# Causal attention into a maxout feed-forward layer: the last query block's two heads transposed by one issue

## The chip, the core and the metric

One core of one Trainium2 chip runs the whole program. The metric is the device time of one execution in microseconds (us); several executions are timed and the median is given. Five engines work side by side: TensorE (PE in the profile; its weight loads are PEld), VectorE (DVE), ScalarE (ACT), GpSimd (POOL) and SyncE (SP), whose queue here issues nearly all the DMA transfers. Each takes its instructions in order, and waits on semaphores for the others.

## The reference, cut to what matters

```python
def attn(q, k, v, s):                      # B, H, S, D = 8, 8, 576, 64
    scores = q @ k^T / sqrt(D)
    cum = cumsum(max(s, 0))
    scores = where(causal, -1e9, scores + min(-(cum[i] - cum[j]), 0))
    p = softmax(scores)                    # with + 1e-9 in the sum
    return p @ v
x = attn(...) as (B*S, H*D) = (4608, 512)
h = max(x @ w1, x @ w2, x @ w3)            # d_ff = 768
out = h @ w_out                            # (4608, 512), float32
```

## The kernel before, in words

**Visits and steps.** Two heads of a batch (a pair) are worked on together; one pair's stay is a visit, and a visit goes through blocks of 128 query rows, one block a step (the last block, number 4, has 64 rows). There are 160 steps: first blocks 0 and 1 of the eight pairs of batches 0 and 1, then their blocks 2, 3 and 4, then all five blocks of the 24 pairs of batches 2 to 7 (the "stacked" visits, with float16 high and low parts of q and k in tiles `h` and `l`). In every step TensorE computes scores two steps ahead, VectorE the row maxima (L738), ScalarE the exponentials, and `probs` (L791) divides by the row sum and splits the result into a float16 high part (`prh`, written by ScalarE) and a low part (`prl`, written by VectorE).

**Transposes.** The product with the values needs the probabilities with the keys on the partitions, so `probs` has SyncE issue DMA transposes into `ph` and `pl`: two issues (high, low) for block 1 (L835), two each for blocks 2 and 3 (L840), and four for block 4 (L846). There the 128 partitions hold 64 rows of each head, and each part of each head is an issue of its own: 64 partitions by 4 blocks (high) or 5 (low, which carries the 64 keys beyond 512 of both parts).

**Values.** `values` (L963) multiplies for a half of a visit: 256 query columns (blocks 0, 1), or 320 (blocks 2, 3, 4) in 28 matmuls. Each takes a 128 x 64 weight tile of one head, so matmuls come in pairs, head 0 and head 1 in different columns of the array. All high parts times the high and low values come first, then the low parts. It runs at the end of the step after the half's last `probs`.

**Feed-forward.** As soon as a batch's half is complete, `add_set` queues 18 up-products (groups of 12 matmuls, L1116, 256 or 320 columns) and 4 down-products (groups of 18, L1158); their results go out by a ScalarE copy (L1166) and one store each (L1167). Batch 0's first half runs in float32 (L1187, L1209). `PLAN["GROUPS"]` says how many groups are run at two places of each step, 309 in all; the rest runs after the last step.

**Order.** Everything else (loads, splits, weight decoding, scales) is put by hand into the list of a step: `at` (L1277) appends to the work at the step's end, shifted by `PLAN["moved"]`, `soon` (L1264) puts it before the scores. Scales need a maximum over the partitions: `power` (L515) is one matmul on a VectorE result (`ambv`, `ambwd`), whose product VectorE reads later. `keep_on` (L908) issues matmuls that compute nothing, as many as `PLAN["KEEP"]` says. For stacked visits `nat_hi`/`nat_lo` (L236, L239) write q and k parts into a staging tile (`fixed`), `nat_own` copies one head's part on the same partitions, and `nat_far` (L268) moves the other by DMA, separately for `h` and `l`.

Of the kernel before, what the change touches and what calls it, by code (L numbers as in the profile page):

```python
# [47 lines left out]
('load_nat', 26): -2, ('nat_far', 38, 1, 0): 1, ('load_nat', 28): -1, ('nat_hi', 24, 0): 1, ('load_nat', 21): -1,
('prep2', 0): -2, ('decode4', 21): 2, ('nat_bias', 36, 0): -1, ('pair_max', 18, 1): 1, ('prep4', 22): -1, ('decode3',
17): -1, ('load_nat', 27): 1, ('nat_bias', 25, 1): 2, ('nat_far', 28, 0, 0): 1, ('prep2', 3): 1, ('prep2', 11): 1,  # L50
('vmax', 39): 1, ('nat_own', 20, 0, 1): 1, ('nat_bias', 22, 1): 2, ('load_v', 31): 1, ('load_nat', 36): -1,
('nat_bias', 35, 1): -2, ('nat_far', 35, 1, 1): 1, ('nat_bias', 38, 1): 1, ('nat_bias', 29, 1): 1, ('nat_hi', 17, 0):
-1, ('prep4', 24): -1, ('prep5', 14): -1, ('nat_hi', 16, 0): -1, ('prep5', 38): 1, ('nat_far', 32, 1, 1): 1,
('nat_own', 31, 0, 1): 1, ('pair_scale1', 2): -1, ('nat_hi', 28, 0): 1, ('nat_far', 32, 1, 0): -1, ('nat_far', 35, 0,
0): -1, ('nat_far', 36, 1, 1): 1, ('bias4', 0): 1, ('nat_far', 21, 1, 1): 1, ('decode4', 22): 1, ('prep4', 35): -2,
('load_w', 10): -1, ('nat_hi', 35, 0): 1, ('load_w', 7): 1, ('nat_hi', 27, 0): -1, ('nat_bias', 24, 0): 1, ('prep3',
6): -1, ('prep5', 24): -1, ('pair_scale3', 4): 1, ('load_nat', 35): -2, ('load_nat', 39): 1, ('nat_own', 35, 1, 0): 2,
('nat_hi', 33, 0): 1, ('nat_bias', 23, 1): 1, ('nat_far', 31, 1, 1): -1, ('prep4', 23): 1, ('nat_far', 29, 1, 0): -1,
('nat_own', 28, 1, 1): 1, ('prep4', 15): -1, ('load_v', 22): -1, ('load_nat', 32): 1, ('load_v', 10): 1, ('nat_far',
35, 1, 0): -1, ('sign', 2): 1, ('sign', 15): 1, ('nat_bias', 26, 1): -1, ('nat_far', 21, 0, 1): 1, ('nat_bias', 28,  # L60
1): -1, ('nat_own', 23, 1, 1): 2, ('prep4', 27): -1, ('load_w', 5): -1, ('nat_far', 28, 1, 0): 1, ('prep4', 9): 1,
('nat_far', 34, 0, 1): -1, ('nat_far', 17, 1, 1): -1, ('prep4', 10): 1, ('nat_bias', 17, 1): -1, ('load_w', 8): -1,
('nat_own', 32, 1, 1): 1, ('nat_own', 31, 1, 1): 1, ('prep2', 15): -1, ('pair_max', 25, 1): 1, ('nat_far', 32, 0, 0):
1, ('prep4', 33): -2, ('prep3', 4): 1, ('decode3', 12): -1, ('prep4', 28): -1, ('prep4', 26): 1, ('nat_hi', 32, 0): 1,
('nat_hi', 18, 1): -1, ('nat_hi', 31, 0): -1, ('nat_own', 27, 0, 1): 1, ('prep4', 38): 2, ('load_nat', 24): -1,
('nat_far', 34, 0, 0): 1, ('vmax', 19): -1, ('prep5', 19): -1, ('pair_max', 17, 0): 2, ('prep4', 29): -1, ('nat_far',
24, 1, 0): -1, ('prep4', 34): -2, ('nat_far', 36, 0, 1): 1, ('vmax', 6): 1, ('nat_bias', 25, 0): -1, ('vmax', 29): 1,
('nat_lo', 38, 1): 1, ('nat_own', 23, 0, 1): 1, ('nat_lo', 29, 0): -1, ('load_nat', 33): -1, ('decode1', 2): -1,
('nat_bias', 31, 1): 1, ('nat_own', 19, 1, 1): 1, ('load_nat', 29): 1, ('prep5', 5): -1, ('prep5', 39): -1,
('nat_far', 18, 0, 1): -1, ('nat_far', 31, 0, 1): -1, ('decode3', 7): -1, ('nat_hi', 39, 1): 1, ('load_v', 26): -1,  # L70
('load_w', 23): -1, ('nat_own', 23, 1, 0): 1, ('nat_bias', 20, 1): 1, ('nat_far', 34, 1, 0): 1, ('gram1', 0, 5): 1,
('nat_hi', 37, 1): 1, ('nat_lo', 34, 0): -1, ('nat_bias', 29, 0): -1, ('nat_far', 37, 1, 1): -1, ('pair_max', 16, 0):
1, ('nat_hi', 21, 0): -1, ('nat_own', 20, 1, 1): 1, ('load_nat', 38): 1, ('nat_lo', 18, 0): -1, ('load_v', 23): -1,
('vmax', 4): -1}),
# [4 lines left out]
"fetched": ({5: 0, 7: -1, 8: 0, 9: 0, 10: -2, 11: 2, 12: 2, 13: 0, 14: 1, 15: 2, 16: 2, 17: 0, 22: 3, 23: 4, 18: 4, 19: 5, 20: 8,  # L79
21: 6}),  # L80
"GROUPS": ([(0, 0), (0, 0), (0, 0), (0, 0), (0, 0), (0, 0), (0, 0), (0, 0), (0, 2), (0, 2), (1, 3), (0, 1), (0, 0), (0, 2), (1,
# [11 lines left out]
"FIRST": (0),  # L93
"KEEP": ({('b', 37): 2, ('d', 69): 10, ('b', 70): 18}),
"EX": ((0, 1, 2)),
"EX0": ((0, 1, 2, 3, 4)),
}
# [1440 lines left out]
```

## Time and profile before

| | us |
|---|---|
| median of 3 runs (846.43 to 849.97) | 848.02 |
| the profiled execution | 846.36 |
| its span, first to last instruction | 844.5 |
| TensorE busy / VectorE / ScalarE / GpSimd | 807.6 / 638.5 / 532.5 / 296.2 |
| granted clock of TensorE, mean | 0.994 |

Busy time is the union of an engine's instructions, so what is left of the span is idle time of that engine. The profiled execution takes 1.9 us more than its span. A matmul's recorded length contains its pipeline and is longer than the distance to the next one's start; distances between starts show the rate.

### The profile page before, as it was taken

To read this page: it belongs to the slowest core of one execution; us is meant where nothing else is said; L and a number is where in the kernel's file an instruction comes from. 1 tells how busy PE (TensorE), PEld (TensorE's weight loads), DVE (VectorE), ACT (ScalarE), POOL (GpSimd) and SP (SyncE) were. 2 spreads that over 40 slices of the span, in tenths; PEclk is the share of its full clock that TensorE was granted. 3 is DMA by queue.
4 is the path that set the end of the run, shared out by engine and by line. 5 is a ranking of instruction groups with operands and counts; after the bars stand their busy time and mean duration, and the time that the engine had idled before them with its cause. 6 is when DMAs were issued, how large, how long until landed. Compare 5 with 4: busy or idle time off the path is not lost.

```text
span 844.5 us, 19376 instructions
## 1 busy us (share of the span) xinstructions
PE 807.6 (96%) x6959; PEld 619.5 (73%) x6959; DVE 638.5 (76%) x1562; ACT 532.5 (63%) x1458; POOL 296.2 (35%) x532
## 2 busy tenths in 40 slices
PE   5889899899999989999999999999999999999998
PEld 3777678777676668777787678777877688778875
DVE  6889988889778888898887879877978787662110
ACT  5878777496577676766775666665766576652111
POOL 1001114757433333254434524362335335221221
PEclk9999899999999999999999999999999999999999
DMA  9933377896877696867886678656787665443000
GB/s 351 378 87 84 84 170 184 184 157 138 160 171 135 127 199 144 172 123 169 186 156 131 124 166 184 137 135 132 143 181 121 128 119 116 92 78 71 19 8 32
DMA packets 236672, 119.82 MB, mean 142 GB/s; under 512 B 208800, under 2 KB 217504, under 8 KB 236576
## 3 DMA queue, kind: packets, MB, share of 16 engines
q1 hardware_dynamic: 236000, 117.01, 63.4%
q10 hardware_dynamic: 576, 1.57, 0.5%
q8 instruction: 55, 0.90, 0.5%
q14 instruction: 41, 0.34, 0.2%
HBM read 45.12 MB, written 9.44 MB: 65 GB/s over the span
## 4 chain that ended last, share of the span: by engine, by line
PE 70%; DVE 11%; DMA 8%; ACT 5%; issue 2%; POOL 2%; SPq 1%; ACTq 0%; DVEq 0%; POOLq 0%
PE pm L1116 40%; PE po L1158 13%; PE av L983 6%; PE s L644 5%; DMA pl<-prl 3%; DVE prl L832 2%; DMA r<-in_w_dram 2%; PE s L656 1%; ACT prh L829 1%; PE pm L1187 1%; DVE w L1089 1%; DMA raw<-in_start_dram 1%; PE po L1209 1%; DMA rv<-in_qkv_dram 1%; ACT e L779 1%
## 5 line engine op out<-in xcount | busy, mean ns | idle before, releaser
L1116 PE MATMUL pm<-x,w 128*128 128x320 f16 (+1 forms) x3240 | 422.4, 287 | 0.9 <-DVE x L994 0.7
L1116 PEld LDWEIGHTS <-w 128*128 128x128 f16 x3240 | 312.2, 98 | 90.2 <-issue 3.5
L829 ACT ACTIVATE prh<-e,ri 128x128 f16<-128x128 f32 (+3 forms) x200 | 96.7, 529 | 95.5 <-DVE ri L807 93.3
L1133 DVE SCALAR_TENSOR_TENSOR m<-pm,m 128x320 f32<-128x320 f32 (+1 forms) x180 | 82.0, 456 | 93.1 <-PE pm L1116 82.6
L1122 POOL CAST hh<-m 128x320 f16<-128x320 f32 (+1 forms) x90 | 46.0, 511 | 298.7 <-DVE m L1133 233.0
L1158 PE MATMUL po<-hh,w 128*128 128x320 f16 (+1 forms) x720 | 140.6, 287 | 0.0
L1158 PEld LDWEIGHTS <-w 128*128 128x128 f16 x1080 | 103.7, 98 | 30.1 <-issue 1.7
L832 DVE SCALAR_TENSOR_TENSOR prl<-e,ri,prh 128x128 f16<-128x128 f32 (+3 forms) x200 | 110.5, 591 | 8.9 <-ACT prh L829 5.7
L748 DVE CUSTOM_DVE_ANT_0 s<-s,later,qf 128x128 f32<-128x128 f32 (+1 forms) x192 | 103.7, 550 | 14.3 <-PE s L644 11.5
L779 ACT ACTIVATE e<-s,nm 128x128 f32<-128x128 f32 (+4 forms) x216 | 105.6, 497 | 5.4 <-DVE nm L748 2.5
L1158 PE MATMUL po<-hl,w 128*128 128x320 f16 (+1 forms) x360 | 103.2, 287 | 0.2 <-POOL hl L1123 0.2
L266 POOL COPY h<-fixed 64x576 f16<-64x576 f16 x96 | 73.2, 778 | 83.2 <-DVE fixed L241 79.2
L1130 ACT ACTIVATE m<-pm 128x320 f32<-128x320 f32 (+1 forms) x90 | 36.4, 405 | 72.5 <-PE pm L1116 69.2
L1123 POOL TENSOR_TENSOR hl<-m,hh 128x320 f16<-128x320 f32 (+1 forms) x90 | 68.7, 764 | 7.4
L829 ACT ACTIVATE prh<-s,ri 128x512 f16<-128x512 f32 x72 | 46.7, 684 | 31.7 <-DVE ri L807 31.6
L1166 ACT ACTIVATE o<-po,os 128x320 f32<-128x320 f32 (+1 forms) x60 | 29.9, 499 | 50.1 <-PE po L1158 44.3
L983 PEld LDWEIGHTS <-vh 128*64 128x64 f16 x800 | 44.9, 110 | 22.3 <-issue 15.4
L832 DVE SCALAR_TENSOR_TENSOR prl<-s,ri,prh 128x512 f16<-128x512 f32 x72 | 51.8, 748 | 8.4 <-ACT prl L829 8.2
L983 PE MATMUL av<-ph,vh 128*64 128x320 f16 (+3 forms) x368 | 48.6, 281 | 1.4 <-DMA ph<-prh 1.4
L779 ACT ACTIVATE s<-s,nm 128x512 f32<-128x512 f32 (+1 forms) x72 | 48.4, 673 | 0.0
L644 PE MATMUL s<-h 128*128 128x128 f16 (+1 forms) x192 | 42.3, 300 | 3.4 <-DVE prl L832 1.8
L241 DVE SCALAR_TENSOR_TENSOR fixed<-fixed,qf,fixed 128x576 f16<-128x576 f32 x48 | 40.6, 881 | 4.7 <-ACT fixed L237 4.7
(210 smaller groups left out, 1202.8 us busy)
## 6 DMA issues: line engine op xcount, KB each, us to landing
fixed<-in_pair_dram SPq DMA_DIRECT2D x24, 576.0 KB, 4.7
r<-in_w_dram SPq DMA_DIRECT2D x22, 512.0 KB, 8.4
rv<-in_qkv_dram SPq DMA_DIRECT2D x32, 320.0 KB, 3.7
h<-fixed SPq DMA_DIRECT2D x48, 144.0 KB, 2.7
l<-fixed SPq DMA_DIRECT2D x48, 144.0 KB, 2.8
out_dram<-o SPq DMA_DIRECT2D x32, 160.0 KB, 2.0
out_dram<-o SPq DMA_DIRECT2D x32, 128.0 KB, 1.9
raw<-in_qkv_dram SPq DMA_DIRECT2D x8, 480.0 KB, 3.9
```

The lines of the kernel that those rows point to most:

```text
L266: nc.gpsimd.tensor_copy(out=R[v]["h"][own, j, x], in_=staged(v)[own, 3 - x])
L644: nc.tensor.matmul(ps[:, j, :nk], lhsT=w[:, c, qs], rhs=w[:, 1 - c, 0:nk], start=(x == "h" and not (lone and j)), stop=(x == "l"), skip_gr ...
L748: nc.vector.tensor_tensor_reduce(out=sc[:, j], in0=sc[:, j], in1=future[0][:, Q4 - nk:Q4], scale=n, scalar=3.0e38, op0=ALU.add, op1=ALU.mi ...
L779: nc.scalar.activation(out=to, in_=sc, func=AF.Exp, bias=nm[:, j:j + 1], scale=-1.0 if below(t) else 1.0, accum_out=sm[:, j:j + 1],)
L829: nc.scalar.activation(out=hi, in_=src, func=AF.Copy, scale=sc)
L832: nc.vector.scalar_tensor_tensor(out=lo, in0=src, scalar=sc, in1=hi, op0=ALU.mult, op1=ALU.subtract)
L983: nc.tensor.matmul(av[j * D:(j + 1) * D, c0:nq] if ph else av[j * D:(j + 1) * D, c0:nq].rearrange("p (i c) -> p i c", c=P), lhsT=lt, rhs=r ...
L1116: nc.tensor.matmul(pm[:, :nq], lhsT=w[:, wt, kt, :], rhs=xt, start=(n == 0), stop=(n == 3 * NKT - 1))
L1122: nc.gpsimd.tensor_copy(out=st["hh"][:, ft, :nq], in_=m1[:, :nq])
L1123: nc.gpsimd.tensor_tensor(out=st["hl"][:, ft, :nq], in0=m1[:, :nq], in1=st["hh"][:, ft, :nq], op=ALU.subtract)
L1133: nc.vector.scalar_tensor_tensor(out=m1[:, :nq], in0=pm[:, :nq], scalar=HSC, in1=m1[:, :nq], op0=ALU.mult, op1=ALU.max)
L1158: nc.tensor.matmul(pm[:, :nq], lhsT=W[18 + ft][:, wt, dt, :], rhs=st[ht][:, ft, :nq], start=(n == 0), stop=(n == 3 * NFT - 1),)
```

## The change

1. **Last block.** `probs` puts both parts of both heads of block 4 into one tile `pr` of 128 x 9 x 128, transposed by one issue into `pT2`; `values` takes the first 256 columns from `ph`, `pl` and then the last 64 from `pT2`, in matmuls of their own: 52 in place of 28.
2. **Far copies.** `h` and `l` of a stacked visit become one tile `lh`; `nat_far` moves both in one issue, at the place of the second.
3. **Stores.** Two down-products share a tile and a store, except in the last set.
4. **Scales.** The `power` matmul of the down weights, and of the values' scale for the visits before the stacked ones, moves from the end of a step to before the scores of the next.
5. **Order.** 60 entries of `moved`, 50 steps of `GROUPS` (309 groups as before), five of `fetched`, and `KEEP` at one step from 10 matmuls to 2.

```diff
-"KEEP": ({('b', 37): 2, ('d', 69): 10, ('b', 70): 18}),
+"KEEP": ({('b', 37): 2, ('d', 69): 2, ('b', 70): 18}),
...
     def nat_far(v, j, x):
+        if not x:
+            return
         own, far = slice(j * D, (j + 1) * D), slice((1 - j) * D, (2 - j) * D)
-        nc.sync.dma_start(out=R[v]["hl"[x]][far, j], in_=staged(v)[own, 1 - x:3 - x])
+        u = staged(v)[own, 0:2]
+        two = bass.AP(tensor=u.tensor, offset=u.offset, ap=[list(u.ap[0]), [S, 2], [1, 2 * S]])
+        nc.sync.dma_start(out=R[v]["lh"][far, :, j].rearrange("p y i c -> p y (i c)"), in_=two)
...
+        elif qb == 4:
+            both = att.tile([P, 9, P], F16, tag="pr4", name=f"pr{t}", bufs=1)
+            halves = [both[:, 0:4], both[:, 4:9]]
...
         elif ph:
-            for c in range(2):
-                for j in range(2):
-                    nc.sync.dma_start_transpose(
-                        out=pT[c][:, 0:8 + 2 * c, 256:320].rearrange("p (n j) c -> p n j c", j=2)[:, :, j, :],
-                        in_=halves[c][j * D:(j + 1) * D, 0:4 + c, :].rearrange("p n c -> p (n c)"),
-                    )
+            nc.sync.dma_start_transpose(out=PT[v, 2], in_=both.rearrange("p n c -> p (n c)"))
...
-                        rt = pT[t][:, 2 * kb + j, c0:nq] if ph else pT[t][:, j + 4 * kb:j + 3 + 2 * kb:2, :]
-                        todo.append((j, r[vt][:, j, kb, :], rt, c0))
+                        rt = pT[t][:, 2 * kb + j, c0:2 * P] if ph else pT[t][:, j + 4 * kb:j + 3 + 2 * kb:2, :]
+                        todo.append((j, r[vt][:, j, kb, :], rt, c0, 2 * P))
         if ph:
+            pT = PT.pop((v, 2))
+            for part in parts:
+                for kb in range(4):
+                    for vt, t in part:
+                        for j in range(2):
+                            todo.append((j, r[vt][:, j, kb, :], pT[:, 4 * t + kb, j * D:(j + 1) * D], 2 * P, nq))
...
-        WS[kind] = power(clamp(am, f"w{kind}"), f"w{kind}")
+        WS[kind] = clamp(am, f"w{kind}")
...
+        if kind == "d" and PLAN["WP"]:
+            soon(end + 1, wscale_power, kind)
...
-        if v < 2 * NP * NB + NP:
+        if v < 2 * NP * NB + NP and PLAN["VP"]:
+            soon(first[v] + 1, vscale_power, scale_of(v))
```

**SyncE's queue at the first stacked visit**, before (`fixed<-in_pair_dram` is a load; the rest as named above):

```order
L840 DMA_TRANSPOSE ph_2712<-prh_2786 128x8x128
L840 DMA_TRANSPOSE pl_2713<-prl_2787 128x8x128
L230 DMA fixed_2854<-in_pair_dram 128x1152
L846 DMA_TRANSPOSE ph_2712<-prh_2884 128x4x64 x2
L846 DMA_TRANSPOSE pl_2713<-prl_2885 128x5x64 x2
L209 DMA rv_2919<-in_qkv_dram 128x640
L270 DMA h_2748<-fixed_2684 64x1152
L270 DMA l_2749<-fixed_2684 64x1152
```

and now:

```order
L856 DMA_TRANSPOSE ph_2802<-prh_2898 128x8x128
L856 DMA_TRANSPOSE pl_2803<-prl_2899 128x8x128
L235 DMA fixed_2951<-in_pair_dram 128x1152
L860 DMA_TRANSPOSE pT_2979<-pr_2982 128x9x128
L214 DMA rv_3012<-in_qkv_dram 128x640
L279 DMA lh_2837<-fixed_2718 64x2x1152 x2
```

Four issues of the last block have become one, and the four far copies (the `h` and `l` rows come twice, once a head) two; the neighbours kept their places.

**TensorE at the scale of the down weights** (`gmwd`; the gram product L1044 that it measures is done), before:

```order
L699 MATMUL s_1092<-kb_180,qr_183 128x384 x2
L703 LDWEIGHTS identb
L703 MATMUL s_1092<-tri,identb 128x128
L519 LDWEIGHTS ambwd
L519 MATMUL gmwd<-identb,ambwd 128x128
L1187 MATMUL pm_0_4_0_1125<-x_0_327,r_361 128x256 x2
L1187 MATMUL pm_0_4_0_1125<-x_0_558,r_361 128x256 x2
```

and now:

```order
L714 MATMUL s_1091<-tri,identb 128x128
L1217 MATMUL pm_0_4_0_1121<-x_0_328,r_362 128x256 x2
L1217 MATMUL pm_0_4_0_1121<-x_0_557,r_362 128x256 x2
L1001 MATMUL av<-ph_939,vh_933 64x256
L1001 MATMUL av<-pl_940,vh_933 64x128
L529 MATMUL gmwd<-identb,ambwd 128x128
L710 MATMUL s_1153<-qk_979 128x512 x6
```

The small matmul that waits for VectorE now stands behind a float32 product of four matmuls and the 12 matmuls of a values half (of which two rows stand for all).

**TensorE's values of a second half**, before, the low parts' last rows:

```order
L983 MATMUL av<-pl_1832,vh_1817 64x320
L983 MATMUL av<-pl_1832,vh_1817 64x192
L983 MATMUL av<-pl_1832,vh_1817 64x64
L983 LDWEIGHTS vl_1818
L983 MATMUL av<-pl_1832,vl_1818 64x64
```

and now:

```order
L1001 MATMUL av<-pl_1920,vh_1868 64x256
L1001 MATMUL av<-pl_1920,vh_1868 64x128
L1001 MATMUL av<-pT_2125,vh_1868 64x64
L1001 LDWEIGHTS vl_1869
L1001 MATMUL av<-pT_2125,vl_1869 64x64
```

The 24 matmuls of 320 or 192 columns have 256 or 128, and 24 of 64 columns, each with a weight load of its own, stand behind them with the four that were there.

## Rows read from the trace of the kernel before

**Rows 1.** Stretches of the span: length, busy us (instructions) per engine, clock, DMA share, GB/s

```profile
core 0: us, PE busy (x) PEld busy (x) DVE busy (x) ACT busy (x) POOL busy (x), PEclk, DMA share, GB/s
0.00:50.00 50.00, 36.04 (x245) 29.53 (x246) 40.02 (x89) 35.41 (x107) 4.21 (x25) 0.97 0.81 309
50.00:130.00 80.00, 72.04 (x460) 57.81 (x458) 68.90 (x151) 59.71 (x154) 10.35 (x12) 0.96 0.50 122
130.00:345.00 215.00, 204.39 (x1839) 154.42 (x1837) 182.13 (x415) 145.34 (x392) 102.54 (x177) 1.00 0.79 158
345.00:772.00 427.00, 426.07 (x3863) 323.12 (x3862) 335.93 (x885) 283.15 (x791) 164.72 (x292) 1.00 0.68 139
772.00:844.50 72.50, 69.07 (x562) 54.64 (x559) 11.49 (x25) 8.84 (x20) 14.36 (x26) 1.00 0.05 17
```

**Rows 2.** Waits of TensorE, all: who waited for whom, us in total, times, longest

```profile
PE av L983 <- DMA pl<-prl: 3.5, 5, 1.7
...
PE gmwd L519 <- DVE ambwd L510: 2.4, 1, 2.4
PE gmv L519 <- DVE ambv L510: 2.3, 2, 1.3
PE s L644 <- DVE prl L832: 1.8, 3, 1.5
...
PE s L644 <- DMA h<-fixed: 1.3, 2, 1.1
```

**Rows 3.** Line 846, its issues: duration ns min/median/max; who waited (us, times); landing

```profile
L846 SPq DMA_TRANSPOSE pl<-prl x64: 1176/1244/2380, 113.2 to 768.2; - x64
...
  PE av L983: 4.4, 7
...
DMA to landing us min/median/max: 2.3/2.4/6.8
```

**Rows 4.** Timeline of SyncE's queue, 138 to 153 us: start, us, what

```profile
140.33 3.19 SPq L840 DMA_TRANSPOSE pl<-prl  x1
143.62 3.57 SPq L846 DMA_TRANSPOSE ph<-prh  x2
147.29 2.50 SPq L846 DMA_TRANSPOSE pl<-prl  x2
```

**Rows 5.** Timeline of TensorE at that visit's values, 148.5 to 152.6 us

```profile
149.86 0.30 PE L983 MATMUL av<-pl,vh 128*64 128x320 f16 x1
151.87 0.65 PE L983 MATMUL av<-pl,vh 128*64 128x320 f16 x8 [1.71 <-DMA pl<-prl]
```

**Rows 6.** Line 840's issues: who waited for them, and landing

```profile
  DVE prl L832: 1.6, 2
...
DMA to landing us min/median/max: 2.7/3.3/6.9
```

**Rows 7.** Timeline of TensorE's far end of a values half, 611.85 to 611.86 us

```profile
611.68 0.20 PE L983 MATMUL av<-pl,vh 128*64 128x64 f16 x2
611.70 0.20 PE L983 MATMUL av<-pl,vl 128*64 128x64 f16 x2
611.84 0.28 PE L1116 MATMUL pm<-x,w 128*128 128x256 f16 x1
```

**Rows 8.** Weight loads by form: count, busy us, mean ns, idle before

```profile
L983 PEld LDWEIGHTS <-vl 128*64 128x64 f16 x432 | 26.4, 110 | 3.5 <-issue 1.3
```

**Rows 9.** Timeline of TensorE, 76 to 96 us

```profile
77.99 5.40 PE L1187 MATMUL pm<-x,r 128*128 128x256 f32 x24
85.84 1.24 PE L1044 MATMUL av<-r 128*128 128x128 bf16 x8 [2.45 <-DVE r L1033]
...
90.61 0.29 PE L519 MATMUL gmwd<-identb,ambwd 128*128 128x128 bf16 x1 [2.41 <-DVE ambwd L510]
90.69 3.73 PE L1187 MATMUL pm<-x,r 128*128 128x256 f32 x8
```

**Rows 10.** Two stretches of 1 us, columns as in rows 1

```profile
91.00:92.00 1.00, 1.00 (x3) 0.81 (x3) 1.00 (x3) 0.31 (x1) 0.00 (x0) 0.50 0.00 0
94.00:95.00 1.00, 1.00 (x11) 0.58 (x12) 1.00 (x2) 0.97 (x3) 0.00 (x0) 0.50 0.00 0
```

**Rows 11.** Issues of far copies and stores: duration ns min/median/max

```profile
L270 SPq DMA_DIRECT2D l<-fixed x48: 462/587/1404, 212.7 to 731.5; - x48
L1167 SPq DMA_DIRECT2D out_dram<-o x60: 332/517/1935, 173.5 to 841.7; - x60
```

**Rows 12.** Waits of VectorE, 95 to 345 us

```profile
DVE prl L832 <- DMA pl<-prl: 2.7, 4, 0.9
```

**Rows 13.** Matmuls that compute nothing: count, busy us, mean ns

```profile
L910 PE MATMUL av<-identb 128*128 128x128 bf16 x30 | 2.0, 219 | 0.0
```

More of the change, by code (lines that the diff above doesn't have):

```diff
@@ L403, in powers @@
         return p2, inv
-    s_t = att.tile([HB, S], F32, tag="qkh", name="s_t")
+    s2_t = att.tile([HB, 2, V0], F32, tag="qk", name="s_t")
+    s_t = s2_t[:, 0, 0:S]
     nc.sync.dma_start(out=s_t, in_=s)
@@ L462, in cumulate @@
     def cumulate():
-        r_t = att.tile([HB, S], F32, tag="qkl", name="r_t")
+        r_t = s2_t[:, 1, 0:S]
         nc.vector.tensor_scalar(out=r_t, in0=s_t, scalar1=0.0, scalar2=None, op0=ALU.max)
@@ L557, in prep2 @@
         if v < NPS:
-            r["q"] = att.tile([P, V0], F32, tag="qkh", name=f"q{v}")
+            r["q"] = att.tile([P, 2, V0], F32, tag="qk", name=f"q{v}")[:, 0]
             nc.scalar.activation(out=r["q"][:, 0:256], in_=r["t"][:, 0:256], func=AF.Copy, scale=SCALE)
@@ L562, in prep2 @@
         cq = c0 + r["q"].shape[1]
-        r["hi"] = att.tile([P, V0], F32R, tag="qkh", name=f"qkh{v}")
+        r["hl"] = att.tile([P, 2, V0], F32R, tag="qk", name=f"qk{v}")
+        r["hi"] = r["hl"][:, 0]
         nc.scalar.activation(out=r["hi"][:, c0:cq], in_=r["q"], func=AF.Copy, scale=SCALE)
@@ L572, in prep3 @@
         cq = c0 + r["q"].shape[1]
-        r["lo"] = att.tile([P, V0], F32R, tag="qkl", name=f"qkl{v}")
+        r["lo"] = r["hl"][:, 1]
         nc.gpsimd.tensor_tensor(
@@ L801, in probs @@
             PT[v, ph] = [
-                att.tile([P, 4 + (4 + 2 * n) * ph, PH[ph][1]] if ph else [P, 6, P], F16, tag=f"pT{c}{ph}", name=f"p{c}{t}", bufs=1)
-                for n, c in enumerate("hl")
-            ]
+                att.tile([P, 8, 2 * P] if ph else [P, 6, P], F16, tag=f"pT{c}{ph}", name=f"p{c}{t}", bufs=1)
+                for c in "hl"
+            ]
+        if qb == 4:
+            PT[v, 2] = att.tile([P, 9, P], F16, tag="pT2", name=f"pT{t}", bufs=1)
         pT = PT[v, ph]
@@ L1164, in ev @@
             def ev():
-                o_t = moe.tile([P, 320], F32, tag="m1", name=f"o{u}_{dt}", bufs=3)
-                nc.scalar.activation(out=o_t[:, :nq], in_=pm[:, :nq], func=AF.Copy, scale=st["os"])
-                nc.sync.dma_start(out=outT[dt * P:(dt + 1) * P, t0:t0 + nq], in_=o_t[:, :nq])
+                lone = (b, ph) == (B - 1, 1)
+                if lone or dt % 2 == 0:
+                    st["o"] = moe.tile([P, 2, 320], F32, tag="o", name=f"o{u}_{dt}", bufs=2)
+                o_t = st["o"][:, 0 if lone else dt % 2, :nq]
+                nc.scalar.activation(out=o_t, in_=pm[:, :nq], func=AF.Copy, scale=st["os"])
+                if lone:
+                    nc.sync.dma_start(out=outT[dt * P:(dt + 1) * P, t0:t0 + nq], in_=o_t)
+                elif dt % 2:
+                    nc.sync.dma_start(
+                        out=outT[(dt - 1) * P:(dt + 1) * P, t0:t0 + nq].rearrange("(a p) n -> p a n", p=P),
+                        in_=st["o"][:, :, :nq],
+                    )
             pending.append(ev)
@@ L1301 @@
         ids = sorted(tiles, key=lambda i: begun[i])
-        scaled[kind] = end = begun[ids[-1]] + 2
+        scaled[kind] = end = begun[ids[-1]] + 2 + (PLAN["DG"] if kind == "d" else 0)
         for n, size in enumerate(parts):
             part = ids[sum(parts[:n]):sum(parts[:n + 1])]
-            t = begun[part[-1]] + 2
+            t = end if n == len(parts) - 1 else begun[part[-1]] + 2
             (soon if t == end else at)(t, gram1, kind, n, part, len(parts))
         at(end, wscale1, kind)
+        if kind == "d" and PLAN["WP"]:
+            soon(end + 1, wscale_power, kind)
+        elif kind == "u" and PLAN["WP"] > 1:
+            soon(end + 1, wscale_power, kind)
+        else:
+            at(end, wscale_power, kind)
     at(scaled["d"] + 1, wscale2, "d")
@@ L1354 @@
             at(t, f, v)
[L1355 removed]
+    at(scaled["u"] + (PLAN["WP"] > 1), wscale2, "u")
     for i, t in split.items():
```

138 lines of the change are left out of this document (73 added, 65 removed), and 16 rows, old and new, of the table PLAN.

## The prediction, written before the change was run

> **What bounds the kernel now.** I read the stretches first, then TensorE's waits, then the timelines at the waits. The stretches [rows 1] show a TensorE that is busy nearly throughout: the stretch lengths less its busy time leave 14.0, 8.0, 10.6, 0.9 and 3.4 us idle, 36.9 us of the span of 844.5. From 345 us on 0.9 us of 427 is left. So TensorE is the bound, and anything that takes work from another engine or queue pays only as far as TensorE waited for it. Nothing in the change touches the first loads or the last set's tail, so the 14.0 and the 3.4 us stay; what can be won lies between 50 and 345 us, at most 8.0 + 10.6 + 0.9 = 19.5 us.
>
> The list of waits [rows 2] names the candidates: values waiting for transposes (3.5 us), two scale products waiting for VectorE (2.4 and 2.3), scores waiting for `prl` (1.8) and for far copies (1.3). The line of the last block's transposes [rows 3] gives its issues 4.4 us in seven waits. At the first stacked visit SyncE's queue runs back to back [rows 4]: from 140.33 to 149.79 us it does nothing but issue six transposes, and the values then stop for 1.71 us on the last low part [rows 5]. VectorE also waits, four times, to overwrite a `prl` that a transpose still reads [rows 12]. Earlier, around 90 us, another loss shows: the gram product waits 2.45 us and `gmwd` 2.41 us [rows 9], and after this idleness the granted clock is 0.50, the lower of its two levels (1.2 of 2.4 GHz) [rows 10].
>
> **The change part by part.** The sum is made against the profiled execution, 846.36 us; the median of the runs is 848.02, so 1.7 us is added at the end.
>
> *A, last block's transposes.* Four issues become one. An issue has a median of 1.24 us [rows 3]; the 128 issues of high and low parts become 32, so 96 x 1.24 = 119 us of SyncE's time goes. What matters is when the last piece lands after VectorE's last write. Before: two low issues one after the other, the second landing 2.4 us after its issue, 1.24 + 2.4 = 3.6 us, and more where the high ones still stood ahead (as in [rows 4], where four take 6.07 us). After: one issue with nine blocks, for which the nearest row is the eight-block form, landing 3.3 us after its issue [rows 6]. So it comes 0.3 us earlier where SyncE was free, and about 4 x 1.24 - 1.24 - (3.3 - 2.4) = 2.8 us earlier where all four stood in line. `values` also asks for it later, behind all 256-column matmuls of the low parts. The seven waits have a mean of 0.63 us and a longest of 1.7; the longest stands in the crowded queue where 2.8 us is gained. Bounds: -4.4 (all waits gone) and 0 (one larger transfer lands as late as the last of the four did). I take -4.4, near the end that the queue's rows give.
>
> Issuing is not the whole path, and **a rule speaks against this part**. The row shows issues of 1.24 us against landings of 2.4 us, with the queue full [rows 3, 4]. The Trainium skill, "DMA: Bandwidth & Descriptors", section "Issuing engines are not separate DMA queues", says that spreading transfers over more issuing engines saves only sequencer time, which is usually small beside the transfer itself. By that, fewer issues would gain little; here the sequencer's time is half the landing, and I go by the row. The other outcome is rival 2.
>
> *B, `prl` and `prh`.* The last block leaves these buffers for a tile of its own, used once a visit. Scores wait 1.8 us for `prl` work [rows 2], and VectorE 2.7 us for the transposes that read the buffers [rows 12]. Bounds -1.8 and 0; I take half, -0.9, since VectorE is busy 182.13 of 215 us in this stretch [rows 1] and may be late for its own work.
>
> *C, scale products.* `gmwd` and the two `gmv` wait 4.7 us together [rows 2]. They now stand behind work that is ready: for `gmwd` a float32 product, of which eight matmuls take 3.73 us at the low clock [rows 9]. The order's rows show that nothing of their step depends on them before. But VectorE is busy 68.90 of 80 us from 50 to 130 us [rows 1], so a TensorE that runs ahead meets it again at the next scores or the next gram product, which keeps its wait of 2.45. Bounds -4.7 and 0; I take half, -2.4.
>
> *D, the low clock.* At the low clock eight float32 matmuls took 3.73 us; 24 at the high one 5.40 [rows 9], so eight 1.80: this stretch cost 1.9 us more. It follows the two idle times, of which C removes one. Bounds -1.9 and 0; I take half, -1.0.
>
> *E, far copies and stores.* Of 96 far copies 48 stay: 48 x 0.59 = 28 us of SyncE's time; some 28 stores fewer save 28 x 0.52 = 15 us [rows 11]. On TensorE's path stand only the scores' waits for `h`, 1.3 us [rows 2]; the queue ahead of them is shorter, but the `h` part now goes at the place of the second copy. Bounds -1.3 and +1.3 (the later place doubles the wait); I take -1.3, as two issues and the transposes' three are gone ahead of it. The rest is hidden: nothing on TensorE waits for a store.
>
> *F, `KEEP`.* Eight empty matmuls fewer, at 2.0 us for 30 [rows 13]: -0.5. They stood where TensorE was idle or slow, so between -0.5 and 0.
>
> *G, the 64-column matmuls.* A values half has 14 pairs before and 26 after, so 12 x 32 = 384 pairs more. Columns are the same: eight matmuls of 320 columns, four pairs, take 0.65 us [rows 5], so 64 columns are a fifth of 0.16, 33 ns, a little of it the pipeline's end. The two 64-column pairs of the old form start at 611.68 and 611.70, about 20 ns apart, so at the rate of their columns [rows 7]. Between the two rows I reckon with 28 ns a pair. But each pair brings new weights, and the same loads have a mean of 110 ns [rows 8]. Loads overlap; whether two dozen in a row do is not shown. Bounds: nothing, and (110 - 28) x 384 = +31.5 us. I take +0.4, one nanosecond a pair, because [rows 7] is the nearest: the same shape, back to back.
>
> Here too **a rule speaks against the change**. The Trainium skill, "TensorE: Matmul & The Clock Gate", section "LDWEIGHTS (loading the stationary operand)", puts a load at its columns over 1.2 GHz, an estimate of 53 ns for 64 columns; if that sets the distance of pairs, G is about +9.6 us. [Rows 7] have less than half of it between two starts, so the trace so far disagrees.
>
> *H, order.* The `moved` and `GROUPS` tables keep the amount of work (309 groups). A TensorE that runs some 9 us earlier meets VectorE and loads sooner. Bounds 0 and +2.6 (twice the `h` waits); I take +1.0.
>
> Sum: -4.4 - 0.9 - 2.4 - 1.0 - 1.3 - 0.5 + 0.4 + 1.0 = -9.1, so 837.3 us for an execution like the profiled one, and **839.0 us** with 1.7 added.
>
> **The rivals.** A measurement of this kernel tells about 0.5% from no change, 4.2 us: below 843.8 is faster, above 852.3 slower.
>
> 1. *All of it.* The waits are independent and the clock never falls: -4.4 - 1.8 - 4.7 - 1.9 - 1.3 - 0.5 + 0.4 = -14.2, so 833.8. For it: DMA and VectorE are both under 90% busy from 130 to 345 us [rows 1]. Against: VectorE before 130 us.
> 2. *Issuing was not what was late.* The DMA engines, 0.79 busy in the stretch of the waits [rows 1], set the landing (up to 6.8 us [rows 3]), and a larger transfer behind the same traffic lands no earlier. A, B and E give nothing: 6.6 less, so 845.6. For it: 0.79. [...]
> 3. *Weight loads become the bound.* Where a 64-column pair cannot start before its two loads are through, each of the 384 new pairs costs up to 110 - 28 = 82 ns, +31.5 in place of +0.4: 870.1. It eats the gain of 9.5 us at (28 + 9500 / 384), about 53 ns a pair, and is slower by 0.5% from about 64 ns. For it: [rows 8]. Against: [rows 7].
> 4. *Loads half hidden.* A pair takes a third of the way from 28 to 110 ns, 55 ns: 384 x 27 = +10.5 us in place of +0.4, so 849.0, no change. For it: the mean of [rows 8] may include waiting, so that a load holds the array for less than 110 ns. Against: [rows 7]. The load rule named under G gives nearly this, 848.2 by its estimate.
>
> **How the numbers follow.** Forecast 0.63, rival 1 0.12, rival 2 0.12, rival 3 0.07, rival 4 0.06. Faster: 0.63 + 0.12 = 0.75; same: 0.12 + 0.06 = 0.18; slower: 0.07. The range goes from 832 (rival 1 and 2 us of the other idle time in 19.5) to 848: it takes in rival 2 and leaves out rivals 3 and 4, 0.13.
>
> **What would show it.** Right: no wait of values for the last block's transpose above 1 us in all; that line with one issue of about 1.3 us a visit; 64-column pairs some 28 ns apart; `gmwd` under 1 us; a granted clock that stays up from 88 to 96 us; and TensorE's idle time from 130 to 345 us down from 10.6 to about 4. Wrong: pairs 50 ns or more apart and a busy TensorE with the same columns in more time (rivals 3, 4); waits for the one transpose of the old size (rival 2); or as much idle time as before under VectorE's names, C and H then being mis-sized.

## The result, and the profile after

| kernel | median, us | ratio to before, 95% interval |
|---|---|---|
| before (6 runs) | 847.22 | 1 |
| changed (6 runs) | 840.42 | 0.9908 [0.9884, 0.9932] |

The change makes the kernel 0.9% faster. The forecast was 839.0 us, in a range from 832 to 848. The profiled execution of the changed kernel has a span of 838.7 us against 844.5, so 5.8 us are to be found in it. The stretches show in which part; the limits stand where those of [rows 1] do, but for the last two, moved with the end.

```profile
0.00:50.00 50.00, 35.79 (x242) 29.49 (x243) 39.77 (x88) 35.13 (x106) 3.92 (x25) 0.97 0.80 308
50.00:130.00 80.00, 72.96 (x477) 58.35 (x477) 69.11 (x153) 59.85 (x154) 10.18 (x12) 0.96 0.50 120
130.00:345.00 215.00, 208.94 (x2189) 161.01 (x2189) 185.42 (x424) 150.42 (x405) 102.72 (x178) 1.00 0.82 163
345.00:766.00 421.00, 419.93 (x4253) 323.10 (x4251) 330.64 (x876) 277.29 (x778) 166.16 (x291) 1.00 0.71 139
766.00:838.70 72.70, 69.36 (x564) 54.89 (x562) 11.49 (x25) 8.88 (x20) 14.36 (x26) 1.00 0.05 17
```

Length less the first busy number is TensorE's idle time: 14.2, 7.0, 6.1, 1.1 and 3.3 us, 31.7 in all against 36.9 before. Of the 5.2 us won 4.5 lie between 130 and 345 us, where the values waited, and only 0.9 between 50 and 130. TensorE's own busy time fell by 0.6 us (807.6 to 807.0).

TensorE's waits of the changed kernel, in the columns of [rows 2] (L1239 and L1217 are the float32 products of batch 0's first half):

```profile
PE s L655 <- DMA lh<-fixed: 2.4, 2, 1.4
PE po L1239 <- DVE h L1229: 2.3, 1, 2.3
PE pm L1217 <- ACT h L1227: 1.8, 2, 1.3
PE s L655 <- DVE prl L848: 1.3, 1, 1.3
...
PE av L1001 <- DMA pl<-prl: 0.2, 1, 0.2
```

Values waited 3.5 us for `pl` before, now 0.2; the waits of `gmwd` and `gmv`, 4.7 us together, are gone from the list. New or larger are the scores' wait for a far copy (1.3 before, 2.4 now) and two waits of the float32 products, `po` for VectorE (0.9 before, 2.3 now) and `pm` for ScalarE (0.5 before, 1.8 now).

SyncE's queue at the first stacked visit, where [rows 4] showed four issues of the last block:

```profile
139.92 4.51 SPq L856 DMA_TRANSPOSE pl<-prl  x1
144.53 1.31 SPq L860 DMA_TRANSPOSE pT<-pr  x1
145.93 0.54 SPq L197 DMA_DIRECT2D raw<-in_qkv_dram  x1
```

The last block's issue starts at 144.53 and is through after 1.31 us; before, four took from 143.62 to 149.79. The line of these issues over the whole run, to be set against [rows 3]:

```profile
L860 SPq DMA_TRANSPOSE pT<-pr x32: 1242/1299/2054, 110.7 to 759.0; - x32
...
who waited for it (us, times):
busy tenths in 40 slices 0000000000000000000000000000000000000000
DMA to landing us min/median/max: 3.2/3.5/6.1
```

The list of who waited for them is empty. One issue takes 1.30 us (predicted about 1.3), and the data lands 3.5 us after the issue (predicted 3.3, from the eight-block form).

### The profile page after: what moved, and what is told of

Read it like the earlier page. It is cut to its first block, busy times and chain, and to the rows that moved or that the text cites. A ratio compares the mean times of both kernels' runs of the same rounds, so it can differ in the third digit from the quotient of the medians.

```text
span 838.7 us, 20489 instructions
## 1 busy us (share of the span) xinstructions
PE 807.0 (96%) x7719; PEld 626.8 (75%) x7719; DVE 636.4 (76%) x1562; ACT 531.6 (63%) x1458; POOL 297.3 (35%) x532
## 4 chain that ended last, share of the span: by engine, by line
PE 79%; DVE 10%; DMA 5%; ACT 3%; issue 1%; POOL 0%; SPq 0%; ACTq 0%; DVEq 0%; POOLq 0%
PE pm L1137 43%; PE po L1179 15%; PE av L1001 7%; PE s L655 6%; DMA r<-in_w_dram 2%; PE s L667 2%; DVE prl L848 2%; PE s L710 1%; PE pm L1217 1%; PE po L1239 1%; DMA lh<-fixed 1%; DVE w L1110 1%; DMA rv<-in_qkv_dram 1%; DMA raw<-in_start_dram 1%; ACT prh L845 1%
## 5 line engine op out<-in xcount | busy, mean ns | idle before, releaser
L845 ACT ACTIVATE prh<-e,ri 128x384 f16<-128x384 f32 (+2 forms) x192 | 91.1, 522 | 82.0 <-DVE ri L820 81.6
L848 DVE SCALAR_TENSOR_TENSOR prl<-e,ri,prh 128x384 f16<-128x384 f32 (+2 forms) x192 | 102.8, 576 | 3.4 <-ACT prh L845 2.4
L271 POOL COPY lh<-fixed 64x576 f16<-64x576 f16 x96 | 73.0, 775 | 80.7 <-DVE fixed L246 78.7
L1144 POOL TENSOR_TENSOR hl<-m,hh 128x320 f16<-128x320 f32 (+1 forms) x90 | 71.2, 791 | 7.4
L655 PE MATMUL s<-lh 128*128 128x128 f16 (+3 forms) x384 | 67.7, 300 | 3.9 <-DMA lh<-fixed 2.4
L1001 PEld LDWEIGHTS <-vh 128*64 128x64 f16 x1312 | 54.3, 111 | 11.7 <-issue 11.1
L655 PEld LDWEIGHTS <-lh 128*128 128x128 f16 x384 | 34.2, 98 | 19.1 <-POOL hl L1144 3.1
L790 ACT ACTIVATION_READ_ACCUMULATOR e<-s,nm 128x1 f32 x216 | 44.0, 204 | 0.0
L1012 DVE SCALAR_TENSOR_TENSOR x<-av,x 128x320 f16<-128x320 f32 (+1 forms) x60 | 27.1, 452 | 20.8 <-ACT x L1011 20.7
```

Source lines behind the costliest of these rows:

```text
L271: nc.gpsimd.tensor_copy(out=R[v]["h"][own, j, x], in_=staged(v)[own, 3 - x])
L655: nc.tensor.matmul(ps[:, j, :nk], lhsT=w[:, c, qs], rhs=w[:, 1 - c, 0:nk], start=(x == "h" and not (lone and j)), stop=(x == "l"), skip_gr ...
L790: nc.scalar.activation(out=to, in_=sc, func=AF.Exp, bias=nm[:, j:j + 1], scale=-1.0 if below(t) else 1.0, accum_out=sm[:, j:j + 1],)
L845: nc.scalar.activation(out=hi, in_=src, func=AF.Copy, scale=sc)
L848: nc.vector.scalar_tensor_tensor(out=lo, in0=src, scalar=sc, in1=hi, op0=ALU.mult, op1=ALU.subtract)
L1001: nc.tensor.matmul(o if ph else o.rearrange("p (i c) -> p i c", c=P), lhsT=lt, rhs=rt, start=(n < 2), stop=(n >= len(todo) - 2), skip_grou ...
```

## The experiments

The times of before are those of runs beside each: 848.03, 847.22 and 848.36 us for the three groups below, so the ratios compare best. Ratios of the twelve runs, with their intervals:

| run | median, us | ratio, 95% interval |
|---|---|---|
| products apart alone, on before | 847.92 | 0.9994 [0.9978, 1.0011] |
| and own tiles, four issues | 844.65 | 0.9964 [0.9945, 0.9983] |
| and two issues | 843.5 | 0.9941 [0.9926, 0.9956] |
| and one issue (the last block alone) | 841.75 | 0.9925 [0.99, 0.995] |
| last block and scales | 838.92 | 0.9887 [0.9872, 0.9902] |
| and paired stores | 838.92 | 0.9896 [0.9878, 0.9914] |
| and merged far copies (tables of before) | 839.04 | 0.989 [0.9866, 0.9913] |
| the same with empty matmuls | 839.73 | 0.9903 [0.9878, 0.9928] |
| changed, far copies apart | 838.18 | 0.988 [0.9855, 0.9906] |
| changed, far copies apart, both late | 838.29 | 0.9876 [0.9858, 0.9894] |
| changed, scales back | 841.29 | 0.9924 [0.9901, 0.9947] |
| changed, four overlapping issues | 864.6 | 1.0201 [1.0167, 1.0235] |

**The last block's products apart, alone.** On the kernel before:

```diff
-    rt = pT[t][:, 2 * kb + j, c0:nq] if ph else ...
+    rt = pT[t][:, 2 * kb + j, c0:2 * P] if ph else ...
...
+    todo.append((j, r[vt][:, j, kb, :], pT[t][:, 2 * kb + j, 2 * P:nq], 2 * P, nq))
```

> The kernel before with the 64-column products apart and last, four issues into the old tiles as before. What the product order alone does. Cost by the changed kernel's trace: 60 ns more in each of 32 second halves, 1.9 us. Theory (issues set the landing): most of the 4.4 us of waits stay, 847 to 850. Rival 'asked later': the waits for the last block fall below 1.5 us, and the time is 844 to 846.5. Rival 'weight loads exposed' stays refuted if a second half takes 1.7 us here too.

TensorE's waits of this kernel:

```profile
PE av L989 <- DMA pl<-prl: 2.0, 3, 0.8
...
PE av L989 <- DMA ph<-prh: 0.5, 1, 0.5
```

The values' waits, 3.5 and 1.4 us for low and high parts before, are 2.5 together; of the 4.4 us for the last block's own transposes 2.0 are left, between what the theory and its rival expected. Asking later is worth 2.4 us of waiting. The time does not move (0.9994). What the new matmuls cost shows in a second half of the changed kernel, of which these are the first row, the middle and the end, and the start of what follows:

```profile
764.08 0.30 PE L1001 MATMUL av<-ph,vh 128*64 128x256 f16 x2
...
765.25 0.20 PE L1001 MATMUL av<-pT,vh 128*64 128x64 f16 x2
765.28 0.20 PE L1001 MATMUL av<-pT,vl 128*64 128x64 f16 x2
765.31 0.20 PE L1001 MATMUL av<-pT,vh 128*64 128x64 f16 x2
...
765.79 1.38 PE L1137 MATMUL pm<-x,w 128*128 128x256 f16 x11
```

Pairs of 64 columns start 0.03 us apart, and the half takes 765.79 - 764.08 = 1.71 us. In the kernel before, the half around [rows 7] takes:

```profile
610.18 0.33 PE L983 MATMUL av<-ph,vh 128*64 128x320 f16 x2
```

to 611.84, that is 1.66 us. So 0.05 us more for 12 more pairs, 32 times 0.05 = 1.6 us (the rows are rounded to 0.01): about 4 ns a pair, where I had taken 1, and not the 110 of a load's own length. A half of the kernel with the products apart alone takes the same 1.71 us (612.94 to 614.65). Rival 3 is out, and with it rival 4.

**Own tiles, and how many issues.** From the last block alone the one issue becomes four; each goes into a tile of its own, and high and low parts come from tiles of their own (the two heads of a part share the source tile, which the expectation overlooks):

```diff
-    both = att.tile([P, 9, P], F16, tag="pr4", ...)
+    halves = [att.tile([P, 4 + c, P], F16, tag=f"pr4{c}", ...) for c in range(2)]
...
-    nc.sync.dma_start_transpose(out=PT[v, 2], in_=both...)
+    for c in range(2):
+        for j in range(2):
+            nc.sync.dma_start_transpose(out=PT[v, 2][c][j], in_=halves[c][j * D:(j + 1) * D]...)
```

(The version with two issues has the loop over `c` alone, 128 partitions each.)

> The kernel before with the first part of the change alone (last block in a tile of its own, one issue, 64-column products apart); far copies, stores, scales and tables as before. Theory: the waits of values for transposes (4.9 us, high and low) go, 60 ns more per second half cost 1.9 us, so 843 to 845. Rival 'tables': the parts need the new order; 846 to 849.

> As the last block alone (841.75 us), but with four issues, each from and into tiles that no other of the four touches, so that none waits for another and the last block still leaves prh and prl free. Only the number of issues differs. Theory (issues set the landing and fill the queue): values wait for the last block's low parts again, 1.5 to 4 us, and 844 to 847. Rival 'own buffers' (the gain comes from the buffers that the last block leaves to the other blocks): waits under 1 us, 841 to 843.

> The kernel before with the last block in tiles of its own and two issues (high of both heads, low of both heads), far copies, stores, scales and tables as before. One issue gave 841.75, four 844.65. Theory (each issue costs queue time): between them, 842 to 844. Rival 'size' (smaller pieces land sooner, 3.8 us against 2.4, and the high part may go before VectorE has written the low one): 840.5 to 841.75 or better than one issue.

With four issues 0.9964, with two 0.9941, with one 0.9925. The intervals of four and one overlap only by 0.0005; that of two overlaps both, so its place between them is not shown. Waits of TensorE for the last block, in the kernel with four issues

```profile
PE av L996 <- DMA pT<-pr: 1.3, 2, 1.0
```

and in the one with one issue only this wait of values for any transpose, of an earlier block:

```profile
PE av L990 <- DMA pl<-prl: 0.3, 1, 0.3
```

So both causes are there. Tiles of its own take the ratio from 0.9994 to 0.9964, and one issue in place of four takes it on to 0.9925, with a median of 841.75 a little below the 843 to 845 that the theory gave. Which of the new tiles counts, that of the source or that of the result, was not tried. Only 1.3 of the 3 us between four issues and one stand in a wait for this tile, so I had the direct part too high (1.5 to 4 us expected).

Where the rest stands is read at the first float32 down-product that waits for VectorE's maximum `h`, with four issues, two and one:

```profile
113.55 0.71 PE L1222 MATMUL po<-h,r 128*128 128x256 f32 x2 [0.85 <-DVE h L1212]
```

```profile
114.09 0.70 PE L1216 MATMUL po<-h,r 128*128 128x256 f32 x2 [0.90 <-DVE h L1206]
```

```profile
112.51 0.71 PE L1216 MATMUL po<-h,r 128*128 128x256 f32 x2 [0.52 <-DVE h L1206]
```

Two issues have the same remainder of the span behind it as one (841.7 - 114.09 = 727.6 and 840.2 - 112.51 = 727.7 us), four have 730.2, and four into the old tiles (the run above) 847.4 - 113.63 = 733.8. So these profiles show 3.6 us for the tiles, 2.5 for one issue or two in place of four, and nothing between two and one. What lies ahead of that point is not the queue's doing. The three kernels do the same work up to there, and the first issue of the last block starts at 112.15 to 112.75 us; but they differ already at a gram product that starts at 74.16, 74.56 and 73.47 us. Before it, from 56 to 58 us, the granted clock was 0.50, 0.50 and 0.64, and from 58 to 60 us 0.77, 0.59 and 1.00. This low stretch follows a wait for `gmv`; more on it under the scales.

**Four issues into the one tile.** The slices that I wrote for the high parts cover blocks 0 to 7 in place of 0 to 3: the high issues carry four of the five low blocks too, and write what the low ones write again.

```diff
-    nc.sync.dma_start_transpose(out=PT[v, 2], in_=both...)
+    for c in range(2):
+        for j in range(2):
+            nc.sync.dma_start_transpose(out=PT[v, 2][:, 4 * c:8 + c, j * D:(j + 1) * D],
+                in_=both[j * D:(j + 1) * D, 4 * c:8 + c]...)
```

> The changed kernel with one step undone: the last block's tile goes out in four issues again (each part of each head, 64 partitions by 4 or 5 blocks), into the same tile, with the same product order. Theory (the number of issues in SyncE's queue set the landing): the values wait again for the last block's transposes, 2 to 4.5 us in all, and the time is 842.5 to 845. Rival 'asked later' (the 64-column products, now last in a values half, no longer need the pieces early, however many issues there are): waits for that tile under 1 us, time 839.5 to 841.5, like the changed kernel's 840.4.

It measures something else than meant, 1.0201, slower than before. SyncE's own waits (its queue, in the columns of the waits):

```profile
SPq L862 <- DVE pr L848: 32.8, 21, 3.7
SPq L862 <- DMA pT<-pr: 31.5, 22, 3.8
```

The low issue now must wait until the high one has landed, and the high one for VectorE's low part. TensorE then waits 14.7 us in 19 places for this tile. It says nothing on the number of issues, but shows what waits at the head of the one queue can do: 24 us lie between this and the changed kernel, of which 14.7 stand in TensorE's waits for this tile. The issues also carry 26 blocks of 64 rows in place of 18; the shares were not separated. It was replaced by the run with own tiles above.

**Scales.** The changed kernel with `"WP": (0)` and `"VP": (0)`, which put the small matmuls back to the step's end:

> The changed kernel with the scale products at their old places (end of the step). Theory (VectorE is the bound from 80 to 110 us, so TensorE only waits elsewhere): the waits of gmwd and gmv come back, 2 to 4.7 us, those for the float32 products (4.1 us) fall by about as much, and the time is 839.5 to 841.5. Rival (the waits were TensorE's own loss): 842.5 to 845.

Measured 841.29 us, inside the theory's range; its ratio of 0.9924 is 0.0016 above the changed kernel's, which the intervals do not tell apart. The waits are back:

```profile
PE gmv L529 <- DVE ambv L520: 3.0, 4, 1.4
...
PE gmwd L529 <- DVE ambwd L520: 1.1, 1, 1.1
```

4.1 us, and the time follows by a fraction. Where they go is read at the same float32 down-product. In the kernel before, in the changed one and in this one:

```profile
111.97 0.71 PE L1209 MATMUL po<-h,r 128*128 128x256 f32 x2 [0.93 <-DVE h L1199]
```

```profile
111.04 0.71 PE L1239 MATMUL po<-h,r 128*128 128x256 f32 x2 [2.27 <-DVE h L1229]
```

```profile
112.01 0.71 PE L1239 MATMUL po<-h,r 128*128 128x256 f32 x2 [0.26 <-DVE h L1229]
```

With the scale products moved TensorE comes to this point early and stands still 2.27 us; with them at the old place it waits there 0.26. It goes on 0.9 to 1.0 us earlier for it, not 2.4. Against the kernel with the scales back this difference of 0.97 us is there long before `gmwd`, at the gram product of 16 matmuls, first in the changed kernel, then with the scales back:

```profile
72.44 2.05 PE L1062 MATMUL av<-r 128*128 128x128 bf16 x16 [0.36 <-DVE x L1012]
```

```profile
73.41 2.05 PE L1062 MATMUL av<-r 128*128 128x128 bf16 x16 [0.31 <-DVE x L1012]
```

From there to the down-product both take 38.60 us, so the later waits, the 1.1 us of `gmwd` among them, cost nothing here. What differs ahead of it is the first `gmv`: with the scales back it waits 1.35 us, until 54.18, and the clock behind it is low. The stretch in the changed kernel, and with the scales back:

```profile
54.00:56.00 2.00, 2.00 (x11) 1.67 (x9) 0.94 (x6) 1.31 (x3) 0.22 (x1) 1.00 0.00 0
54.00:56.00 2.00, 1.82 (x5) 1.54 (x6) 1.18 (x7) 1.07 (x2) 0.22 (x1) 0.50 0.00 0
```

**The low clock.** The changed kernel with the tables of before, and 40 empty matmuls of 64 columns that no result uses ahead of the gram product that waits 2.45 us:

```diff
-"KEEP": ({('b', 37): 2, ('d', 69): 10, ('b', 70): 18}),
+"KEEP": ({('b', 37): 2, ('d', 69): 10, ('e', 14): 40, ('b', 70): 18}),
...
+            if t == end:
+                soon(t, hold, "e", t)
```

> The changed kernel with the tables of before (839.0 us) and 40 empty 64-column matmuls ahead of the gram product that waits 2.45 us for VectorE, about 2.3 us of work in an idle time of 2.45. They compute nothing that is used. Theory 'low clock is a loss of its own': the clock stays at 1.0 from 86 to 95 us and eight float32 matmuls take 1.9 us in place of 3.8; 836.5 to 838. Rival 'VectorE is the bound there': the clock stays up, but TensorE waits later for VectorE, 838.5 to 839.5.

```profile
84.44 1.33 PE L919 MATMUL av<-identb 128*128 128x64 bf16 x40 [0.64 <-DVE x L1010]
86.25 1.24 PE L1060 MATMUL av<-r 128*128 128x128 bf16 x8 [0.48 <-DVE r L1049]
...
89.64 3.64 PE L1215 MATMUL pm<-x,r 128*128 128x256 f32 x8 [1.03 <-ACT h L1225]
...
111.29 0.71 PE L1237 MATMUL po<-h,r 128*128 128x256 f32 x2 [1.88 <-DVE h L1227]
```

The 40 took 1.33 us, 33 ns each and not the 58 I had reckoned, so they fill half of the idle time. The scores behind it ran sooner, then TensorE waited 1.03 us for ScalarE's `h`, and the clock fell after that wait: the eight float32 matmuls still take 3.64 us. A clock that stays up, which both sides took for granted, was not reached, so its worth is open; but the down-product starts at 111.29 us, and without the empty matmuls it started at 111.25:

```profile
111.25 0.71 PE L1237 MATMUL po<-h,r 128*128 128x256 f32 x2 [1.28 <-DVE h L1227]
```

What TensorE gains ahead of 111 us is taken back there. In this the rows bear out the rival (839.73 us, just above its 838.5 to 839.5).

**Far copies.** Apart again at their two places (the lines of the diff undone), and apart but both at the later place:

```diff
     def nat_far(v, j, x):
         if not x:
             return
...
+        for y in range(2):
+            nc.sync.dma_start(out=R[v]["hl"[y]][far, j], in_=staged(v)[own, 1 - y:3 - y])
```

> The changed kernel with the far copies of h and l as issues of their own, h at its earlier place. Theory (the later place of h is what scores waited 2.4 us for; the saved issues hide elsewhere): waits of scores for far copies fall to under 1.3 us, 839 to 840.5. Rival (48 issues less in the queue are worth something): other waits for DMA grow and the time is 841.5 to 844.

> The changed kernel with the far copies as two issues, both at the later place: the place of the change with the size of before. Theory 'size' (one larger copy lands 4.1 us after its issue in place of 2.8): scores wait under 1 us for them, 837.5 to 839.5. Rival 'place' (h is asked for before it can land): the 2.4 us of waits stay, 840 to 841.5.

Measured 0.988 (838.18 us, less than expected) and 0.9876 (838.29, as theory 'size' expected). Apart at two places no wait of scores for a copy is left on the list; apart and late 0.3 us is. The second is the fastest kernel of the study by its ratio, [0.9858, 0.9894] against [0.9884, 0.9932] of the changed one; the intervals just overlap, so that it beats the change is likely and not shown. The landing times, of the changed kernel and of the one with both late:

```profile
L279 SPq DMA_DIRECT2D lh<-fixed x48: 598/612/1768, 206.1 to 724.0; - x48
...
  PE s L655: 2.4, 2
...
DMA to landing us min/median/max: 3.2/4.1/7.0
```

```profile
L278 SPq DMA_DIRECT2D lh<-fixed x96: 461/588/1828, 206.5 to 723.6; - x96
...
  PE s L654: 0.3, 1
...
DMA to landing us min/median/max: 2.3/2.8/4.8
```

One copy of double size lands 4.1 us after its issue, two of single size 2.8 each, at the same place. So size does it, not place. The merged copy saves an issue of 0.59 us; its data comes 1.3 us later than that of the first of two, and about 0.7 later than that of the second (an estimate: 4.1 - 0.59 - 2.8).

**Tables, stores.** The tables of before in the changed kernel; then also the far copies apart; then also each store its own:

> The changed kernel with the tables of before (moved, fetched, GROUPS, and 10 empty matmuls in KEEP). Theory (the parts of the code carry the gain, the tables are worth within 1.5 us): 839 to 842. Rival 'tables' (the work was placed anew so that nothing waits, and that is the gain): 844 to 847, with waits of scores and products between 130 and 345 us back to some 10 us of idle TensorE.

> The changed kernel with the tables of before and the far copies apart: what is left is the last block, the scale products and the paired stores. Theory (tables worth nothing, merged far copies a loss): 837 to 839.5, as with the far copies apart alone (838.2), and no wait of scores for a far copy. Rival (the new tables are what made the separate copies land in time): scores wait again over 1 us for them, 840 to 842.

> The changed kernel with the tables of before, the far copies apart, and every store its own again in the old tiles: the last block and the scale products alone are left. Theory (nothing on TensorE's path waits for a store): within 1 us of the same kernel with paired stores, 837 to 839.5. Rival (28 issues of 0.52 us less in SyncE's queue let transposes go earlier): 840 to 843, with waits of values for DMA.

0.989, 0.9896 and 0.9887: all one, and none worse than the changed kernel. The new tables bring nothing that these runs can tell, and neither do paired stores. In the old order the merged copies cost nothing either: scores wait 0.2 us for them. So the late landing of the merged copy costs only where the order asks for it early: in the changed kernel at two scores, those after 324.7 and 664.5 us. The last block and the scale products alone, 0.9887, hold the whole gain (with the one tile that `h` and `l` share); the parts of the change beside them are worth nothing or a little less.

## Why the prediction was right, point by point

The side and the size came out: -9.1 us forecast for the sum, -7.8 by the ratio (0.0092 of 847.22), -6.8 by the two medians. That the sum came within 1.4 us is in part luck: B gave more than its price, while the gain of E did not come.

- **A and B, the last block** (-4.4 and -0.9, with G +0.4: -4.9). Alone it measures 0.9925, -6.4 us of 848 (interval -8.5 to -4.2). Right: the waits for the last block are gone, from a queue with one issue instead of four. By the ratios its own tiles have a share of 0.9994 to 0.9964, 2.5 us, and the number of issues one of 0.9964 to 0.9925, 3.3 us, both with wide intervals. I had priced the tiles at -0.9, so B is the term that was sized too small. VectorE's waits to overwrite `prl` [rows 12] are gone from its list between 95 and 345 us; the scores' waits for `prl` only fell from 1.8 to 1.3. Rival 2, by which A, B and E give nothing, is out. The Trainium skill, "DMA: Bandwidth & Descriptors", section "Issuing engines are not separate DMA queues", calls the sequencer's time usually small beside the transfer. For far copies and stores these runs agree (nothing gained from 48 and 28 fewer issues); for the last block, whose four issues stood ahead of a waiting TensorE, they do not (four 0.9964, one 0.9925).
- **C and D, scales and clock** (-2.4 and -1.0). The waits fell by all of 4.7, and the point where TensorE meets VectorE again came 0.9 us earlier (111.97 to 111.04). This was named as what would make C smaller, and it did. D is the step that failed: a granted clock that stays up from 88 to 96 us was forecast as its sign, and it is not there. Eight float32 products at the low clock took 3.73 us before [rows 9], and take 3.63 now:

```profile
88.71 3.63 PE L1217 MATMUL pm<-x,r 128*128 128x256 f32 x8
```

  What the moved products did end stands elsewhere, near 54 us, where the profile before happens to show a clock of 1.00. In the five other kernels with `gmv` at its old place the clock is 0.50 or 0.51 from 54 to 56 us, and the gram product of 16 matmuls starts at 73.20 to 74.56 us (72.09 before). In the eight with `gmv` moved it starts at 72.28 to 73.13; three of them show a low clock there too, for a shorter time. And another low stretch has come, after the longer wait for VectorE at 111 us. The stretches of 1 us, columns as in [rows 10]:

```profile
88.00:89.00 1.00, 1.00 (x11) 0.75 (x8) 1.00 (x4) 0.10 (x1) 0.00 (x0) 0.87 0.49 183
91.00:92.00 1.00, 1.00 (x4) 0.59 (x2) 1.00 (x3) 0.73 (x2) 0.00 (x0) 0.50 0.13 49
113.00:114.00 1.00, 1.00 (x4) 0.84 (x4) 1.00 (x3) 0.10 (x1) 0.00 (x0) 0.50 1.25 230
116.00:117.00 1.00, 1.00 (x6) 0.87 (x6) 0.04 (x1) 0.00 (x0) 0.00 (x0) 0.97 0.69 282
```

  By the ratios the scales are worth between 0.0016 (undone in the changed kernel) and 0.0038 (added to the last block), 1.4 to 3.2 us (the second with the tile that `h` and `l` share); the intervals don't say more.
- **E, far copies** (-1.3). Wrong in sign: scores' waits for them rose by 1.1 us (1.3 to 2.4). I had taken the end of the gain for the shorter queue, and the other end for the later place; what counted was that a copy of twice the size lands 4.1 us after its issue in place of 2.8. That paired stores hide was right.
- **F** was too small to see. **G** was 1.6 us rather than 0.4: pairs start about 32 ns apart, where I had reckoned with 28 and one more. The Trainium skill, "TensorE: Matmul & The Clock Gate", section "LDWEIGHTS (loading the stationary operand)", puts a load at its columns over 1.2 GHz, an estimate of 53 ns for such a load. The trace disagrees that this sets the distance: fourteen pairs in a row, two loads each, start within 0.41 us (765.25 to 765.66), about 32 ns apart.
- **H, order** (+1.0). New stalls came (2.3 us for `po` against 0.9, 1.8 for `pm` against 0.5), 2.7 us more together. But they belong to the moved scale products, not to the order: with the tables of before these two waits are 2.7 to 3.4 us in all, and with the new tables and the scales back 0.3. What the tables add is the low clock behind the longest of these waits. The twelve float32 down-products there, in the changed kernel and with the tables of before:

```profile
113.06 4.29 PE L1239 MATMUL po<-h,r 128*128 128x256 f32 x12
```

```profile
113.14 2.81 PE L1237 MATMUL po<-h,r 128*128 128x256 f32 x12
```

  That is 1.5 us, near the 1.0 forecast, and near the difference of the ratios (0.9908 and 0.989), which the intervals do not tell apart.
- TensorE's idle time from 130 to 345 us went to 6.1, not to 4; a wait of 1.4 us for a far copy and 1.3 for `prl` are the largest that are left there.

## What to carry to other kernels

When one queue issues everything, look at the issues that stand between a producer's last write and the waiting engine, and merge those, in tiles that nothing else waits for; merging transfers elsewhere here saved issues that nobody waited for, and made each land later. An early gain on the bound engine counts only up to the next place where it meets another engine: find that instruction, and compare its start in both traces before believing a sum of waits. Compare two profiles from a point up to which both kernels do the same work: five such kernels reach the gram product at 72.09 to 74.56 us, a spread as large as the parts that were to be told apart. Try each part of a large change alone: here two of five hold all of it.

## What was not expected

One transfer of 288 KB landed 4.1 us after its issue and two of half the size 2.8 us each, although the larger one moved the same rows at the same place. Forty 64-column matmuls, each with a 128 x 128 weight load of its own, took 33 ns each in a row, though the loads of their line have a median of 98 ns: a load's recorded length is not what it adds. And 24 us, more than three times what the whole change gains, were lost with a wrong slice that made issues of one queue wait for each other and carry more. The low clock near 54 us, which decided how early the float32 products ran, was not in the profile on which the prediction was built.
